# A fused attention and two-layer MoE kernel: the opening stage re-planned, with a shorter root for the norm

## The chip, the cores and the metric

The kernel runs on one core of a Trainium2 chip. The metric is device time in microseconds (us), the median of three runs. The profile is one further execution taken by the hardware profiler. The engines are PE (TensorE, the matmuls), DVE (VectorE), ACT (ScalarE), POOL (GpSimd) and SP (SyncE, which here issues the DMA transfers).

## The reference

Three layers follow each other. Linear attention over 4 batches, 8 heads, 576 positions and head size 64, with a norm over each head; then an expansion from 512 to 2048 features and back with an ELU between (`w_in`, `w_out`); then four experts of 1024 features weighted by probabilities (`w1`, `w2`).

```
kv  = einsum('bhsd,bhse->bhde', k, v)
out = einsum('bhsd,bhde->bhse', q, kv)
x   = out / sqrt(mean(out * out, axis=-1) + 1e-6) * g_norm     # per head
h   = x @ w_in;  g = where(h > 0, h, exp(min(h, 0)) - 1);  y = g @ w_out
out = sum_e p[:, e] * (max(y @ w1[e], 0) @ w2[e])               # p: probabilities over their sum
```

`w_in` and `w_out` arrive as 64-bit floats; the kernel converts them on the chip.

## The kernel before, in words

The 2304 tokens are 18 tiles of 128 rows, and six blocks (0 to 5) of three tiles. Large products are taken in three matmuls (high part by high, high by low, low by high) of float32r tiles, so every operand has to be split: ACT casts the high part (`nc.scalar.copy` in `split`), POOL subtracts it to get the low part.

For each block the opening stage does, in this order: `emit_o` (q times the kv of its batch, three PSUM banks, PE), `emit_square` (ACT), `emit_sum` and `emit_norm` (DVE: sum over a head, then the reciprocal root by a starting value in integer arithmetic and three Newton steps), `emit_scale` (DVE), `emit_xT` (PE transposes), `emit_x` (ACT writes the high part of the transposed block, DVE the low part). Then come `product1` (PE, one chunk of 128 features of `w_in`, 12 matmuls into bank a or b in turn), `begin_elu` (ACT), `end_elu` (DVE, which reads the bank of `product1` for the last time), `split_h` (ACT cast, POOL subtraction), and `half` (PE, 12 matmuls with `w_out` for two of the four output columns), whose banks `half_acc` copies out on ACT. Only chunks 0 and 1 of `w_in` and `w_out` are used in this stage. `emit_kv` accumulates k^T v of a tile (PE) and `emit_kvd` copies a batch's result out (ACT); `emit_o` of tiles 9 to 11 needs that of batch 2.

The conversion of a 64-bit chunk, `plan_float32`, has five pieces with places of their own: `begin_float32` (DVE, two instructions on the raw chunk, L151 and L154), `hold_exponent` (ACT, two), `add_low` (DVE, L168), `end_float32` (DVE, L176 and L179) and the split (ACT and POOL). Raw chunks lie in two buffers.

What sets the order: every piece is put into a list with a number (`at_place`), block j from 20 j on; the list is sorted and written out, and the instructions of PE, DVE, ACT and POOL are then tied to that order by dependencies that wait for nothing. Each of the four engines runs its instructions in that order. The order of SP's transfers is chosen by the scheduler. `busy(n)` gives PE n matmuls whose result nobody reads. After the opening stage come the other chunks of the expansion, with an order chosen by the scheduler, and then the experts.

Of the kernel before, what the change touches and what calls it, by code (L numbers as in the profile page):

```python
# [8 lines left out]
F32 = mybir.dt.float32  # L9
F32R = mybir.dt.float32r  # L10
AF = mybir.ActivationFunctionType
ALU = mybir.AluOpType
U32 = mybir.dt.uint32
# [11 lines left out]

@with_exitstack  # L30
def attention_moe_kernel(
# [14 lines left out]
    nc = tc.nc  # L46
    P = 128
    NT, DM = out.shape
    D, = g_norm.shape
    H = DM // D  # L50
# [12 lines left out]
    TT = T // P  # L63
# [26 lines left out]
    cv_p = layer1.enter_context(tc.tile_pool(name="cv", bufs=2, side="right"))  # L90
# [13 lines left out]
    g_sb = const.tile([P, 1], F32, name="g_sb")  # L104
    g8 = const.tile([P, 1], F32, name="g8")
# [40 lines left out]
    def begin_float32(r):  # L146
        r = r.rearrange("p (f t) -> p f t", t=2)
        w_low, w_high = r[:, :, 0], r[:, :, 1]
        m = cv_p.tile([P, 512], U32, tag="m", name="m")
        x = cv_p.tile([P, 512], U32, tag="x", name="x", bufs=1)  # L150
        nc.vector.tensor_scalar(  # L151
            out=x, in0=w_high, scalar1=20, scalar2=0x7FF, op0=ALU.logical_shift_right, op1=ALU.bitwise_and
        )
        nc.vector.tensor_scalar(  # L154
            out=m, in0=w_high, scalar1=0xFFFFF, scalar2=0x100000, op0=ALU.bitwise_and, op1=ALU.bitwise_or
        )
        return w_low, w_high, m, x
# [130 lines left out]
    at_p = at.enter_context(tc.tile_pool(name="at", bufs=2))  # L288
# [5 lines left out]
    for b in range(NKVD):  # L294
        t = at_p.tile([P, NHP, P], F32, tag=f"kvd{b}", name="kvd", bufs=1)
# [29 lines left out]
    ps_o, sums, xs = {}, {}, {}  # L325
# [24 lines left out]
    def emit_norm(j):  # L350


        s = sums[j]
        y, t = (at_p.tile([P, TT, H], F32, tag=n, name=n, bufs=1) for n in ("y", "t"))
        ts, tt, stt = nc.vector.tensor_scalar, nc.vector.tensor_tensor, nc.vector.scalar_tensor_tensor
        nc.vector.tensor_scalar_add(s, s, D * 1e-6)
        ts(out=y.bitcast(U32), in0=s.bitcast(U32), scalar1=-0.5, scalar2=float(0x5F3759DF), op0=ALU.mult, op1=ALU.add)
        for n in range(3):
            stt(out=t, in0=s, scalar=-0.5, in1=y, op0=ALU.mult, op1=ALU.mult)
            tt(out=t, in0=t, in1=y, op=ALU.mult)  # L360
            stt(out=s if n == 2 else y, in0=t, scalar=1.5, in1=y, op0=ALU.add, op1=ALU.mult)

    def emit_scale(t):

# [211 lines left out]
    def load_g():  # L576
        for o in (0, D):
            nc.sync.dma_start(out=g_sb[o:o + D], in_=g_norm.rearrange("(d o) -> d o", o=1))
        nc.gpsimd.tensor_scalar_mul(g8, g_sb, float(D)**0.5)

    def loads(text):
        for n in text.split():
# [10 lines left out]
    def at_place(place, op, *args):  # L593
        plan.append((place, len(plan), op, args))
# [3 lines left out]
    def plan_float32(ab, c, begins, holds, adds, ends, splits):  # L598
        def begin():
            load_w(0, ab, c)  # L600
            parts_of[ab, c] = begin_float32(raws[0, ab, c])

        def end():
            parts_of[ab, c] = end_float32(parts_of[ab, c])

        at_place(begins, begin)
        at_place(holds, lambda: hold_exponent(parts_of[ab, c]))
        at_place(adds, lambda: add_low(parts_of[ab, c]))
        at_place(ends, end)
        at_place(splits, lambda: split_w(0, ab, c, parts_of.pop((ab, c))))  # L610
# [22 lines left out]
    plan_norm(range(TT), [(-20, -19, -18, -10, -9.8, -7), (-19.5, -18.5, -17.5, -9.6, -8.8, -6),  # L633
                          (-19.2, -18.2, -17.2, -9.2, -7.8, -5)], ("abd", "fgh"))
    at_place(-16, emit_norm, 0)
    for place, op, n in ((-15, emit_kv, 5), (-14, emit_kv, 6), (-13, busy, 4), (-7.5, emit_kv, 7), (-7.4, emit_kv, 8)):
        at_place(place, op, n)
    at_place(-4.5, emit_kvd, 1)
    plan_float32(0, 1, -17.8, -17.1, -9, -4, -3.9)
# [3 lines left out]
    for j in range(NB):  # L643
        z = 20 * j
        if j + 1 < NB:
            plan_norm(range(TT * (j + 1), TT * (j + 2)), [
                (z, z + 1, z + 1.6, z + 6.5, z + 11.1, z + 11.4),
                (z + .9, z + 1.9, z + 2.5, z + 7.2, z + 11.6, z + 12.0),
                (z + 1.8, z + 2.8, z + 3.4, z + 7.9, z + 12.1, z + 12.6),
            ], ("dgh", "dgh"))  # L650
            at_place(z + 4.1, emit_norm, j + 1)
        first, second = ((2.7, 4.9, 8.4), (6.9, 8.3, 10.5)) if j else ((-.1, .3, 1.5), (6.9, 7.2, 8.2))
        for c, (mm, begins, ends) in enumerate((first, second)):
            at_place(z + mm, product1, j, c)
            at_place(z + begins, begin_elu, j, c)
            at_place(z + ends, end_elu, j, c)
            at_place(z + ends + (2 if j + c == 0 else 0), split_h, j, c)
        for t in more_kv.get(j, ()):
            at_place(z + 9, emit_kv, *t)
        if j in (1, 2):  # L660
            at_place(z + 9.3, emit_kvd, j + 1)
        if j:
            at_place(z + (4.8 if j > 1 else 12.6), half, j - 1, (0, 1))
            at_place(z + (6.5 if j > 1 else 12.65), half_acc, j - 1, (0, 1))
            at_place(z + 13.1, half, j - 1, (2, 3))
            at_place(z + 14.5, half_acc, j - 1, (2, 3))
        if j == NB - 2:
            at_place(z + 14, end_attention)
    plan_float32(1, 0, .1, 3, 12.7, 12.8, 12.9)
    plan_float32(1, 1, 28.9, 29, 29.1, 30.6, 30.61)  # L670
    plan_float32(0, 2, 48.9, 49, 49.1, 54, 54.1)
    plan_float32(0, 3, 68.9, 69, 69.1, 74, 74.1)
    plan_float32(1, 2, 100, 100.1, 100.2, 103, 103.1)
    plan_float32(1, 3, 108.9, 109, 109.1, 114, 114.1)
    z = 20 * NB
    at_place(z, half, NB - 1, (0, 1))
    at_place(z + 1, half_acc, NB - 1, (0, 1))
# [31 lines left out]
    for g, cs in list(enumerate(first_groups))[1:]:  # L709
        begins = 2 * len(steps)  # L710
# [17 lines left out]
    for h in range(2 * (len(steps) + LAG)):  # L728
        s, second = divmod(h, 2)
# [99 lines left out]
```

## Time and the profile before

| | |
|---|---|
| median of 3 runs | 1237.86 us (1237.55 to 1238.34) |
| the profiled execution, its own time | 1235.05 us |
| its span, first to last instruction | 1233.3 us |
| PE busy | 1207.3 us, 98% of the span |
| DVE, ACT, POOL busy | 51%, 36%, 28% |

The page of the profile gives busy time by engine and by groups of instructions; the trace behind it can be asked for waits, for stretches and for single instructions. Busy PE time counts matmuls at either of the two clock levels, so the granted clock is to be read beside it: 1.00 is 2.4 GHz and 0.50 is 1.2 GHz.

### The profile page before, as it was taken

Reading aid. Unit: us, or ns where it says so; the run is one execution under the profiler, and the core shown is the slowest. Engines: PE = TensorE matmul, PEld = TensorE weight load, DVE = VectorE, ACT = ScalarE, POOL = GpSimd, SP = SyncE. Lnnn points to the kernel's source line nnn. Section 1 sums busy time; section 2 is a strip of 40 time slices with the busy share of each in tenths; the row PEclk is TensorE's granted clock in tenths of the full one; section 3 lists DMA queues with packets and bytes.
Section 4 is the critical chain, followed back from the end, with each engine's and each line's share of the span. In section 5 each row is a group of like instructions: output and inputs, shape, how many; then the busy total and the mean of one; then the engine's idle time right before and its main releaser. Section 6 shows DMA issues by size and latency. Waiting matters only on the chain.

```text
span 1233.3 us, 16894 instructions
## 1 busy us (share of the span) xinstructions
PE 1207.3 (98%) x6656; PEld 1123.2 (91%) x6656; DVE 628.7 (51%) x1089; ACT 444.4 (36%) x858; POOL 339.9 (28%) x296
## 2 busy tenths in 40 slices
PE   8798999999999999999999999999999999999998
PEld 7698999999999999999999999999999999999997
DVE  5766897565222524855445445445444444444443
ACT  3566766544344443342122123123123123222110
POOL 1212444344233644343023023023023022121000
PEclk9799999999999999999999999999999999999999
DMA  9511323110000311542451451451551551550562
GB/s 333 206 44 52 89 84 103 52 52 18 1 10 12 137 66 45 230 155 57 179 192 47 178 203 37 185 205 35 188 205 35 188 200 34 193 197 18 205 231 77
DMA packets 43887, 147.14 MB, mean 119 GB/s; under 512 B 7072, under 2 KB 7072, under 8 KB 43808
## 3 DMA queue, kind: packets, MB, share of 16 engines
q1 hardware_dynamic: 43808, 146.07, 33.7%
q8 instruction: 52, 0.85, 0.3%
q14 instruction: 27, 0.22, 0.1%
HBM read 124.82 MB, written 21.23 MB: 118 GB/s over the span
## 4 chain that ended last, share of the span: by engine, by line
PE 84%; DVE 8%; DMA 3%; ACT 2%; issue 2%; POOL 1%; SPq 0%; DVEq 0%; ACTq 0%; POOLq 0%
PE ps_y L546 11%; PE ps_y L545 11%; PE ps_y L547 11%; PE ps_h L413 4%; PE ps_h L412 4%; PE ps_h L414 4%; PE ps_y L452 4%; PE ps_y L451 4%; PE ps_y L450 4%; PE ps_a L492 3%; PE ps_c L493 3%; PE ps_a L494 3%; PE ps_c L494 3%; PE ps_a L493 3%; PE ps_c L492 3%; PE ps_b L493 3%
## 5 line engine op out<-in xcount | busy, mean ns | idle before, releaser
L546 PE MATMUL ps_y<-w,h 128*128 128x512 f32 x576 | 226.2, 393 | 0.0
L545 PE MATMUL ps_y<-w,h 128*128 128x512 f32 x576 | 223.9, 391 | 0.4 <-DVE acc L558 0.4
L547 PE MATMUL ps_y<-w,h 128*128 128x512 f32 x576 | 220.2, 391 | 0.0
L531 DVE SCALAR_TENSOR_TENSOR h<-c,h 128x384 fp32r<-128x384 f32 x144 | 97.9, 680 | 135.7 <-ACT h L530 135.7
L519 POOL TENSOR_TENSOR c<-u,p 128x384 f32<-128x384 f32 x48 | 48.7, 1014 | 423.2 <-DVE h L531 423.2
L184 POOL TENSOR_TENSOR h<-e,h 128x384 fp32r<-128x384 f32 x96 | 101.1, 1055 | 200.2 <-ACT h L183 173.6
L530 ACT ACTIVATE h<-c 128x384 fp32r<-128x384 f32 x144 | 75.6, 525 | 202.2 <-POOL c L519 76.7
L412 PE MATMUL ps_h<-x,w 128*128 128x384 f32 x384 | 130.0, 339 | 3.8 <-DVE e L426 3.1
L413 PE MATMUL ps_h<-x,w 128*128 128x384 f32 x384 | 128.6, 335 | 0.9 <-DVE x L388 0.9
L452 PE MATMUL ps_y<-h,w 128*128 128x384 f32 x384 | 129.1, 337 | 0.3 <-POOL w L184 0.3
L451 PE MATMUL ps_y<-h,w 128*128 128x384 f32 x384 | 129.0, 336 | 0.0
L450 PE MATMUL ps_y<-h,w 128*128 128x384 f32 x384 | 123.3, 338 | 5.3 <-ACT w L183 4.3
L414 PE MATMUL ps_h<-x,w 128*128 128x384 f32 x384 | 128.4, 334 | 0.0
L547 PEld LDWEIGHTS ps_y<-w,h 128*128 128x128 f32 x576 | 108.1, 188 | 21.7
L545 PEld LDWEIGHTS ps_y<-w,h 128*128 128x128 f32 x576 | 108.0, 188 | 19.5 <-DVE acc L558 0.8
L546 PEld LDWEIGHTS ps_y<-w,h 128*128 128x128 f32 x576 | 108.0, 188 | 19.5
L558 DVE SCALAR_TENSOR_TENSOR acc<-ps_y,p_sb,acc 128x512 f32<-128x512 f32 x126 | 87.6, 746 | 65.2 <-PE ps_y L547 64.9
L426 DVE SCALAR_TENSOR_TENSOR e<-e,ps_h 128x384 f32<-128x384 f32 x96 | 52.5, 548 | 115.1 <-ACT e L422 112.7
L421 ACT ACTIVATE e<-ps_h 128x384 f32<-128x384 f32 x96 | 46.8, 487 | 93.0 <-PE ps_h L414 89.1
L412 PEld LDWEIGHTS ps_h<-x,w 128*128 128x128 f32 x384 | 72.1, 188 | 6.9 <-DVE e L426 5.9
L508 ACT COPY p<-ps_c 128x384 f32<-128x384 f32 x48 | 23.1, 481 | 153.2 <-PE ps_c L494 153.2
L450 PEld LDWEIGHTS ps_y<-h,w 128*128 128x128 f32 x384 | 72.2, 189 | 6.3 <-ACT w L183 4.6
(103 smaller groups left out, 2375.7 us busy)
## 6 DMA issues: line engine op xcount, KB each, us to landing
f<-kept SPq DMA_DIRECT2D x98, 768.0 KB, 7.6
raw<-in_moe_w_dram SPq DMA_DIRECT2D x64, 256.0 KB, 2.7
kept<-f SPq DMA_DIRECT2D x21, 768.0 KB, 3.8
raw<-in_moe_w_in_dram SPq DMA_DIRECT2D x16, 512.0 KB, 3.7
raw<-in_moe_w_out_dram SPq DMA_DIRECT2D x16, 512.0 KB, 3.6
qkv<-in_k_dram SPq DMA_DIRECT2D x18, 256.0 KB, 5.7
qkv<-in_v_dram SPq DMA_DIRECT2D x18, 256.0 KB, 5.8
qkv<-in_q_dram SPq DMA_DIRECT2D x18, 256.0 KB, 5.8
```

The lines of the kernel that those rows point to most:

```text
L184: eng.tensor_tensor(out=lo, in0=src, in1=hi.bitcast(F32), op=ALU.subtract)
L412: nc.tensor.matmul(ps, ah, bh, start=(kk == 0), stop=False)
L413: nc.tensor.matmul(ps, ah, bl, start=False, stop=False)
L414: nc.tensor.matmul(ps, al, bh, start=False, stop=(kk == KD - 1))
L450: nc.tensor.matmul(ps, bh[:, cols], hi, start=first, stop=False)
L451: nc.tensor.matmul(ps, bh[:, cols], lo, start=False, stop=False)
L452: nc.tensor.matmul(ps, bl[:, cols], hi, start=False, stop=last)
L493: nc.tensor.matmul(ps, wh, xl, start=False, stop=False, skip_group_check=True)
L531: nc.vector.scalar_tensor_tensor(out=lo, in0=ps, scalar=0.0, in1=hi.bitcast(F32), op0=ALU.max, op1=ALU.subtract,)
L545: nc.tensor.matmul(ps, hi[:, cols], bh, start=first, stop=False)
L546: nc.tensor.matmul(ps, hi[:, cols], bl, start=False, stop=False)
L547: nc.tensor.matmul(ps, lo[:, cols], bh, start=False, stop=last)
```

## The change

The root takes two Newton steps in place of three (another starting value, constants that make up for it, a factor in `g8`), and its two scratch tiles become slices of the tile of squares. The scratch tile `x` of the conversion has two buffers in place of one. The rest is places: two more idle-time `busy` calls are set in block 0 (9, and 6 in place of 4); in blocks 0 and 1 `emit_kv` comes ahead of the transposes; the transposes (`emit_xT`) and `emit_x` come about two places earlier; `split_h` has a place of its own, behind `emit_x`; the second `end_elu` of a block comes behind `emit_x`; in block 0 the first one does too. Both early chunks of `w_out` are converted in block 0; before, the second one was converted in block 1.

```
-        x = cv_p.tile([P, 512], U32, tag="x", name="x", bufs=1)
+        x = cv_p.tile([P, 512], U32, tag="x", name="x")
...
-        y, t = (at_p.tile([P, TT, H], F32, tag=n, name=n, bufs=1) for n in ("y", "t"))
+        y, t = (xs[TT * j + TT - 1][:, n:n + TT, :H] for n in (0, TT))
...
-        ts(out=y.bitcast(U32), in0=s.bitcast(U32), scalar1=-0.5, scalar2=float(0x5F3759DF), op0=ALU.mult, op1=ALU.add)
-        for n in range(3):
-            stt(out=t, in0=s, scalar=-0.5, in1=y, op0=ALU.mult, op1=ALU.mult)
+        ts(out=y.bitcast(U32), in0=s.bitcast(U32), scalar1=-0.5, scalar2=float(0x5F1FFFF9), op0=ALU.mult, op1=ALU.add)
+        for scale, add, into in ((-1.0, ROOT_ADD, y), (-0.5 * ROOT_MUL**2, 1.5, s)):
+            stt(out=t, in0=s, scalar=scale, in1=y, op0=ALU.mult, op1=ALU.mult)
             tt(out=t, in0=t, in1=y, op=ALU.mult)
-            stt(out=s if n == 2 else y, in0=t, scalar=1.5, in1=y, op0=ALU.add, op1=ALU.mult)
+            stt(out=into, in0=t, scalar=add, in1=y, op0=ALU.add, op1=ALU.mult)
...
-    for place, op, n in ((-15, emit_kv, 5), (-14, emit_kv, 6), (-13, busy, 4), (-7.5, emit_kv, 7), (-7.4, emit_kv, 8)):
+    for place, op, n in ((-15.5, busy, 9), (-15, emit_kv, 5), (-14, emit_kv, 6), (-13, busy, 6),
+                         (-7.5, emit_kv, 7), (-7.4, emit_kv, 8)):
...
-                (z, z + 1, z + 1.6, z + 6.5, z + 11.1, z + 11.4),
-                (z + .9, z + 1.9, z + 2.5, z + 7.2, z + 11.6, z + 12.0),
-                (z + 1.8, z + 2.8, z + 3.4, z + 7.9, z + 12.1, z + 12.6),
+                (z, z + 1, z + 1.6, z + 6.5, z + 9.0, z + 10.4),
+                (z + .9, z + 1.9, z + 2.5, z + 7.2, z + 9.2, z + 10.8),
+                (z + 1.8, z + 2.8, z + 3.4, z + 7.9, z + 9.4, z + 11.2),
...
-        first, second = ((2.7, 4.9, 8.4), (6.9, 8.3, 10.5)) if j else ((-.1, .3, 1.5), (6.9, 7.2, 8.2))
+            (2.7, 4.9, 8.4, 11.4) if j else (-.1, 3.5, 11.6, 11.6), (6.9, 10 if j else 8.3, 11.5, 11.7)
...
-            at_place(z + ends + (2 if j + c == 0 else 0), split_h, j, c)
+            at_place(z + splits, split_h, j, c)
         for t in more_kv.get(j, ()):
-            at_place(z + 9, emit_kv, *t)
+            at_place(z + (9.8 if j > 1 else 8.95), emit_kv, *t)
         if j in (1, 2):
-            at_place(z + 9.3, emit_kvd, j + 1)
+            at_place(z + 12, emit_kvd, j + 1)
         if j:
-            at_place(z + (4.8 if j > 1 else 12.6), half, j - 1, (0, 1))
-            at_place(z + (6.5 if j > 1 else 12.65), half_acc, j - 1, (0, 1))
+            at_place(z + (4.8 if j > 1 else 8.9), half, j - 1, (0, 1))
+            at_place(z + (6.5 if j > 1 else 10.3), half_acc, j - 1, (0, 1))
...
-    plan_float32(1, 0, .1, 3, 12.7, 12.8, 12.9)
-    plan_float32(1, 1, 28.9, 29, 29.1, 30.6, 30.61)
-    plan_float32(0, 2, 48.9, 49, 49.1, 54, 54.1)
-    plan_float32(0, 3, 68.9, 69, 69.1, 74, 74.1)
+    plan_float32(1, 0, .1, 4.6, .2, 11.45, 11.5)
+    plan_float32(1, 1, .3, 4.7, 11.46, 11.47, 11.8)
+    plan_float32(0, 2, 48.9, 51.6, 49, 53.9, 54)
+    plan_float32(0, 3, 68.9, 71.6, 69, 73.9, 74)
     plan_float32(1, 2, 100, 100.1, 100.2, 103, 103.1)
-    plan_float32(1, 3, 108.9, 109, 109.1, 114, 114.1)
+    plan_float32(1, 3, 108.9, 109, 109.1, 114, 114.6)
```

Three places of the order carry the argument. The first is DVE between block 0's low parts and block 1's sums. Before (`raw_130` is chunk 1 of `w_in`, `raw_258` chunk 0 of `w_out`, `sq_400` block 1's first tile of squares, `e_388` the ELU of block 0's first chunk):

```order
L176 SCALAR_TENSOR_TENSOR x_265<-raw_130,x_265 128x512
L179 SCALAR_TENSOR_TENSOR m_264<-m_264,x_265 128x512
L151 TENSOR_SCALAR x_385<-raw_258 128x512
L154 TENSOR_SCALAR m_384<-raw_258 128x512
L426 SCALAR_TENSOR_TENSOR e_388<-e_388,ps_h_355 128x384
L348 TENSOR_REDUCE ss_403<-sq_400 128x8
```

In the change, where all lines are three or four further down (`raw_380` is chunk 1 of `w_out`, `sq_409` block 1's first tile of squares):

```order
L179 SCALAR_TENSOR_TENSOR x_265<-raw_130,x_265 128x512
L182 SCALAR_TENSOR_TENSOR m_264<-m_264,x_265 128x512
L154 TENSOR_SCALAR x_392<-raw_258 128x512
L157 TENSOR_SCALAR m_391<-raw_258 128x512
L171 SCALAR_TENSOR_TENSOR m_391<-raw_258,m_391 128x512
L154 TENSOR_SCALAR x_397<-raw_380 128x512
L157 TENSOR_SCALAR m_396<-raw_380 128x512
L351 TENSOR_REDUCE ss_411<-sq_409 128x8
```

The first two instructions on chunk 1 of `w_out` now stand ahead of block 1's sums, and the first ELU's end is gone from here. The order of SP's transfers up to this chunk is the same in both kernels; it is its 45th.

The second place is DVE behind block 1's scaling. Before (`ps_xT_506` is the last transposed tile of block 1, `e_449` the second ELU of block 0, `sq_529` block 2's first tile of squares):

```order
L366 TENSOR_TENSOR sq_413<-ps_o_405,ss_403 128x512
L426 SCALAR_TENSOR_TENSOR e_449<-e_449,ps_h_435 128x384
...
L388 SCALAR_TENSOR_TENSOR x_496<-ps_xT_506,g8_93,x_496 128x4x128
L168 SCALAR_TENSOR_TENSOR m_384<-raw_258,m_384 128x512
L176 SCALAR_TENSOR_TENSOR x_385<-raw_258,x_385 128x512
L179 SCALAR_TENSOR_TENSOR m_384<-m_384,x_385 128x512
L348 TENSOR_REDUCE ss_531<-sq_529 128x8
```

In the change (`ps_xT_493` is that last tile, `e_424` and `e_455` are the first and the second ELU of block 0):

```order
L392 SCALAR_TENSOR_TENSOR x_507<-ps_xT_493,g8_93,x_507 128x4x128
L179 SCALAR_TENSOR_TENSOR x_392<-raw_258,x_392 128x512
L182 SCALAR_TENSOR_TENSOR m_391<-m_391,x_392 128x512
L171 SCALAR_TENSOR_TENSOR m_396<-raw_380,m_396 128x512
L179 SCALAR_TENSOR_TENSOR x_397<-raw_380,x_397 128x512
L182 SCALAR_TENSOR_TENSOR m_396<-m_396,x_397 128x512
L430 SCALAR_TENSOR_TENSOR e_455<-e_455,ps_h_440 128x384
L430 SCALAR_TENSOR_TENSOR e_424<-e_424,ps_h_362 128x384
L351 TENSOR_REDUCE ss_545<-sq_543 128x8
```

Both ends of block 0's ELUs now stand behind five conversion instructions; the bank that `e_424` reads is the one that block 1's first `product1` writes next.

The third place is ACT around block 4's high parts (the x written from ps_xT). Before:

```order
L421 ACTIVATE e<-ps_h 128x384
L422 ACTIVATE e<-e 128x384
L183 CAST h<-e 128x384
L162 ACTIVATE x<-x,ebias 128x512
L163 ACTIVATE x<-x,ebias 128x512
L183 CAST h<-e 128x384
L387 ACTIVATE x<-ps_xT,g_93 128x4x128 x3
```

In the change:

```order
L425 ACTIVATE e<-ps_h 128x384
L426 ACTIVATE e<-e 128x384
L391 ACTIVATE x<-ps_xT,g_93 128x4x128 x3
L186 CAST h<-e 128x384
L165 ACTIVATE x<-x,ebias 128x512
L166 ACTIVATE x<-x,ebias 128x512
L186 CAST h<-e 128x384
```

The two casts of h, the second of which needs the end of an ELU on DVE, and the two conversion instructions have moved from ahead of the high parts to behind them.

## Rows read from the trace of the kernel before

**Rows 1.** Busy time by engine in three stretches; then granted clock, DMA.

```profile
36.00:64.00 28.00, 20.71 (x128) 18.74 (x129) 19.77 (x39) 13.39 (x25) 5.54 (x5) 0.76 0.44 155
64.00:112.00 48.00, 44.37 (x356) 41.60 (x355) 34.45 (x80) 30.39 (x59) 8.60 (x8) 1.00 0.13 39
112.00:300.00 188.00, 185.59 (x1058) 182.89 (x1058) 133.27 (x227) 112.92 (x217) 81.86 (x70) 1.00 0.23 71
```

**Rows 2.** PE's waits between 36 and 64 us: in total, times, longest.

```profile
PE ps_y L450 <- ACT w L183: 4.3, 1, 4.3
```

**Rows 3.** PE's waits between 64 and 112 us.

```profile
PE ps_o L334 <- DVE x L388: 2.3, 1, 2.3
PE ps_h L413 <- DVE x L388: 0.5, 1, 0.5
PE ps_h L412 <- ACT x L387: 0.4, 1, 0.4
```

**Rows 4.** Busy time in two stretches of 2 us; third from the end the clock.

```profile
38.00:40.00 2.00, 1.41 (x8) 0.83 (x7) 0.84 (x2) 1.13 (x3) 0.54 (x1) 0.66 1.03 377
44.00:46.00 2.00, 2.00 (x13) 2.00 (x13) 0.82 (x2) 1.62 (x4) 1.27 (x1) 0.64 0.45 131
```

**Rows 5.** SP's queue: start, duration, transfer.

```profile
32.05 0.33 SPq L137 DMA_DIRECT2D raw<-in_moe_w_out_dram  x1
```

**Rows 6.** DMA issues between 32.0 and 32.5 us: size, us to landing.

```profile
raw<-in_moe_w_out_dram SPq DMA_DIRECT2D x1, 512.0 KB, 5.9
```

**Rows 7.** DVE in order of time: start, us, line, operation, count, idle before.

```profile
28.41 0.42 DVE L154 TENSOR_SCALAR m<-raw 128x512 uint32<-128x512 uint32 x1
...
40.00 2.07 DVE L388 SCALAR_TENSOR_TENSOR x<-ps_xT,g,x 128x512 fp32r<-128x512 f32 x3 [1.17 <-ACT x L387]
...
42.59 0.68 DVE L176 SCALAR_TENSOR_TENSOR x<-raw,x 128x512 uint32<-128x512 uint32 x1
...
51.59 0.54 DVE L426 SCALAR_TENSOR_TENSOR e<-e,ps_h 128x384 f32<-128x384 f32 x1
...
52.84 1.47 DVE L168 SCALAR_TENSOR_TENSOR m<-raw,m 128x512 f32<-128x512 uint32 x1
...
83.30 1.87 DVE L348 TENSOR_REDUCE ss<-sq 128x8 f32<-128x512 f32 x3 [1.95 <-ACT sq L341]
85.20 0.18 DVE L356 TENSOR_SCALAR ss<-ss 128x24 f32<-128x24 f32 x1
...
87.66 1.89 DVE L366 TENSOR_TENSOR sq<-ps_o,ss 128x512 f32<-128x512 f32 x3
```

**Rows 8.** PE in order of time.

```profile
37.24 2.17 PE L377 MATMUL ps_xT<-ident,sq 128*128 128x128 f32 x12 [1.62 <-DVE sq L366]
40.81 5.14 PE L334 MATMUL ps_o<-kvd,qkv 128*128 128x128 f32 x24 [1.40 <-DVE x L388]
45.71 0.42 PE L412 MATMUL ps_h<-x,w 128*128 128x384 f32 x1
...
50.05 1.30 PE L315 MATMUL ps_kv<-qkv 128*64 128x64 f32 x32
...
64.03 2.84 PE L334 MATMUL ps_o<-kvd,qkv 128*128 128x128 f32 x24
...
75.67 1.53 PE L377 MATMUL ps_xT<-ident,sq 128*128 128x128 f32 x12
...
88.40 1.85 PE L377 MATMUL ps_xT<-ident,sq 128*128 128x128 f32 x12
```

**Rows 9.** ACT in order of time.

```profile
53.97 0.73 ACT L322 COPY kvd<-ps_kv 64x256 f32<-64x256 f32 x2
...
92.69 0.51 ACT L183 CAST h<-e 128x384 fp32r<-128x384 f32 x1 [0.76 <-DVE e L426]
93.10 1.84 ACT L387 ACTIVATE x<-ps_xT,g 128x512 fp32r<-128x512 f32 x3
```

**Rows 10.** POOL in order of time.

```profile
52.76 1.01 POOL L184 TENSOR_TENSOR h<-e,h 128x384 fp32r<-128x384 f32 x1 [6.77 <-ACT h L183]
```

More of the change, by code (lines that the diff above doesn't have):

```diff
@@ L14 @@
 AX = mybir.AxisListType
+ROOT_MUL, ROOT_ADD = 0.703952253, 2.38924456
 @with_exitstack
@@ L578, in load_g @@
             nc.sync.dma_start(out=g_sb[o:o + D], in_=g_norm.rearrange("(d o) -> d o", o=1))
-        nc.gpsimd.tensor_scalar_mul(g8, g_sb, float(D)**0.5)
+        nc.gpsimd.tensor_scalar_mul(g8, g_sb, float(D)**0.5 * ROOT_MUL * (1 + 3.26e-7))
     def loads(text):
@@ L646, in attention_moe_kernel @@
             plan_norm(range(TT * (j + 1), TT * (j + 2)), [
-                (z, z + 1, z + 1.6, z + 6.5, z + 11.1, z + 11.4),
-                (z + .9, z + 1.9, z + 2.5, z + 7.2, z + 11.6, z + 12.0),
-                (z + 1.8, z + 2.8, z + 3.4, z + 7.9, z + 12.1, z + 12.6),
+                (z, z + 1, z + 1.6, z + 6.5, z + 9.0, z + 10.4),
+                (z + .9, z + 1.9, z + 2.5, z + 7.2, z + 9.2, z + 10.8),
+                (z + 1.8, z + 2.8, z + 3.4, z + 7.9, z + 9.4, z + 11.2),
             ], ("dgh", "dgh"))
             at_place(z + 4.1, emit_norm, j + 1)
-        first, second = ((2.7, 4.9, 8.4), (6.9, 8.3, 10.5)) if j else ((-.1, .3, 1.5), (6.9, 7.2, 8.2))
-        for c, (mm, begins, ends) in enumerate((first, second)):
+        for c, (mm, begins, ends, splits) in enumerate((
+            (2.7, 4.9, 8.4, 11.4) if j else (-.1, 3.5, 11.6, 11.6), (6.9, 10 if j else 8.3, 11.5, 11.7)
+        )):
             at_place(z + mm, product1, j, c)
```

## The prediction

> **What bounds the kernel now.** I read the stretches first. PE is busy in almost all of the span, and behind 112 us it stands for 2.4 us of 188 [rows 1]; so the change can only win what PE loses ahead of that, and lose by making PE stand. From 36 to 64 us PE is busy for 20.7 of 28 us, and its mean clock is 0.76: (1 - 0.76) / 0.5 x 28 = 13.4 us lie at the lower level, where each matmul takes twice as long. From 64 to 112 us the clock is 1.00 and PE stands for 3.6 us. Then I read what PE waits for: up to 64 us for the cast of `w_out` chunk 1 (4.3 us, its conversion ends too late, [rows 2]) and for the scaled tile of block 1 (1.62, [rows 8]); from 64 to 112 us chiefly for the parts of x: 2.3, 0.5 and 0.4 [rows 3]. Last I followed the chain of single instructions on DVE, ACT and PE through blocks 0 to 5; the steps below come from there.
>
> **Block 1: the wait that the change makes.** It lets DVE begin `w_out` chunk 1 ahead of block 1's sums. That chunk's transfer is issued at 32.05 and lands 5.9 us later, at 38.0 [rows 5, 6]. Its place on SP is the same in the change, and the DMA engines are still full at 38 to 40 us (share 1.03, [rows 4]), so I take 38.0 again. DVE is past chunk 0's first pair at 28.8 [rows 7]; with the new `add_low` (0.7) it stands from about 30 to 38. Behind the waiting instruction are block 1's sums, root and scaling, and for these PE waits. What block 0 gains or loses ahead of that (three root instructions less, 11 more `busy` matmuls) is swallowed: whichever way, DVE is at the transfer in time.
>
> The Trainium skill ("TensorE: Matmul & The Clock Gate", engine queue depths) says that Vector and Scalar queues are strictly first in, first out and only TensorE pulls weight loads ahead. By that nothing passes the waiting instruction, which speaks against the change; the sum as worked out here is the same, and without the rule it would be that of the hidden transfer below. No row here shows an overtaking on DVE.
>
> From 38.0, with durations from [rows 7] unless said:
> - the pair on chunk 1, 2 x 0.42: 38.8; three sums, 1.9: 40.7
> - the root: 11 instructions take 87.66 - 85.20 = 2.46, so 8 take 1.8: 42.5. The strided slices cost nothing, as the low part, which is written in pieces of 128, costs 0.69 a tile, like the plain 128x512 (0.68). Were each to cost double, it would be 1.8 more
> - the first scaled tile, 0.6, and 0.1 to PE: 43.2. PE has then stood since 35.6 (before, until 37.24, [rows 8]), and the clock has fallen: after that shorter stand it fell at 38.6 (a mean of 0.66 from 38 to 40) and came back at 45.4 (0.64 from 44 to 46) [rows 4]
> - transposes at the low clock: 24 records of `emit_o` took 5.14 there [rows 8], so 12 take 2.6: 45.8
> - last high part 0.6 [rows 9], low part 0.7, handing over 0.3: 47.4
> - conversions in between: five instructions of about 0.7, and 0.6 because one falls beside POOL's split of chunk 0 (beside POOL such an instruction took 1.47, [rows 7, 10]): 51.5
> - two ends of ELUs, 0.5 each: 52.5
>
> Only now is bank a free for block 1's `product1`. PE has done `emit_o` (24 records at 5.14 / 24 = 0.21 while the clock is low, at 2.84 / 24 = 0.12 behind, [rows 8]) by about 49.5, and stands once more, for about 3 us. Before, that product began at 45.71 [rows 8]. So here the change is 6.8 us late.
>
> It then gets most of this back, since the 4.3 us wait and the low stretch around it are gone. Two products last 50.05 - 45.71 = 4.3 [rows 8], so half of one pair is 2.1. From 52.5: two products 56.8, `half` 58.9, k^T v 1.2 (1.30 with its tail): 60.1, where block 2's transposes begin. Chunk 1 of `w_out` is split by 56.6 (its cast is behind two of h, and POOL needs about 1.0 for each piece, [rows 10]), in time. Behind the transposes stands a new wait: `emit_o` of tiles 9 to 11 needs batch 2's copy, which now lies on ACT behind three high parts and both casts of h, the second of which needs an ELU's end behind the low parts. That is 0.8 to the first high part (a third of 1.53 for the tile, [rows 8], and handing over), 1.8 for three, 0.8 for the last low part, 0.5 for the ELU, 0.5 for the cast, 0.7 for the copy [rows 7, 9]: 5.2, against 3.6 of PE work. So `emit_o` starts at 65.3 with a full clock, against 64.03 [rows 8]: **+1.3**.
>
> The clock: before, it stayed up over a stand of 2.3 us [rows 1, 3] and fell over the 4.3 [rows 1, 2]. A stand of 3 us, short after a low stretch, lies between; I take it as falling, being third in a row of gaps. The low stretches before lasted 6.7 us (two in 13.4); of the one after the stand about half falls on work, 3.2 us, which costs half of that: **+1.6**. Bounds: 0 (no fall) and 3.4 (all 6.8 on work). So `emit_o` of block 3 starts at 66.9, 2.9 late.
>
> **Blocks 3 to 5: the waits that the change takes away.** Before, ACT ran block 4's high parts at 93.10, behind a cast that had waited for an ELU [rows 9], while their transposes had been there since 88.4 to 90.3 [rows 8]. The change puts high and low parts directly behind the transposes, with 2.1 us of `half` between them and their user, and k^T v as well behind the transposes of block 3. High parts and low parts are done 3.4 us after the transposes begin (0.8 + 1.8 + 0.8); transposes and `half` take 1.5 + 2.1 = 3.6. So the waits of [rows 3] go, and with them the 3.6 us in which PE stood [rows 1]. A stop also costs the overlap of matmuls (24 start 4.34 / 24 = 0.18 apart, while the one after a stop lasts 0.42, [rows 8]): 0.2 for each of some four stops, 0.7. The transposes of blocks 4 and 5 were drawn out by waits within them, 1.85 against 1.53 [rows 8]: 2 x 0.32 = 0.6. Together **-5.0** (bounds: -2.5 if the waits are only halved, and -5.0, for no more can go). The shorter root is worth nothing here: PE's other work covers it, as the scaled tile is ready about 1 us ahead of the transposes. Were that cover gone it would be 0.65 a block.
>
> **Behind 112 us.** The scheduler's order changes in many places. PE stands there for 2.4 us while DVE is busy for 133 of 188 [rows 1], and a second `x` buffer lets DVE's conversions overlap: bounds -2.4 and, with DVE worse placed, the same standing half as long again, +1.2; I take **-0.6**, nearer to nothing since DVE's work stays the same.
>
> **Sum.** 1.3 + 1.6 - 5.0 - 0.6 = -2.7. Of the profiled execution's 1235.05 us (span 1233.3 and 1.75 around it) that leaves 1232.35; it ran 2.8 below the median, which goes to 1237.86 - 2.7 = **1235.2**.
>
> **The rivals.**
> - *No second fall of the clock.* The stand before block 1's products is met at full clock: 1.6 less, 1233.6. For it: 2.3 us did not make it fall. Against: the stand is longer. 0.15.
> - *The transfer is hidden.* If chunk 1 lands by 31, block 1's scaled tile is there at 37.2 as before [rows 8] and not at 43.2, 6.0 earlier: 1229.2. Against it stands the landing at 38.0 on full DMA engines. 0.05.
> - *The clock stays low through blocks 1 and 2* (the other side). The stands before the transposes, before the products and before block 3's `emit_o` follow each other; if the clock does not return between them, work of 11 us runs at half speed. Each us of it beyond my 3.2 costs what it would have taken: up to 8 more, 1243; from 5.1 more on the kernel is slower than before by over 0.2%. For it: 13.4 us at the low level before, with fewer stands. Against: full PE work brought the clock back at 45.4. 0.15. The Trainium skill (the same page, on oscillation of the clock in real kernels) says that gaps let the array fall back to half rate and that each burst then starts cold. By that this rival gains weight; the trace agrees in its two low stretches [rows 1, 4].
> - *The waits of blocks 3 to 5 only move.* The ELU's first end and `begin_float32` still stand ahead of the low parts on DVE; if high and low parts come 1 us later than reckoned, half of the 5.0 stays: 1237.7. 0.20.
>
> **How the numbers follow.** Forecast 0.45, with its own range 1233.6 to 1236.8. A measurement of this kernel tells about 0.2%, 2.5 us, from no change: faster is below 1235.4, slower above 1240.3. Of the forecast 0.27 lies below 1235.4 and 0.18 above. Faster: 0.27 + 0.15 + 0.05 = 0.47; the same: 0.18 + 0.20 = 0.38; slower 0.15. The range takes in the first rival, the fourth and the near part of the third: 1231.6 to 1240.0, leaving out the hidden transfer and most of the third.
>
> **What would show it.** Right: DVE standing until about 38 on an instruction that reads raw, PE standing 7 us ahead of block 1's transposes and 3 us ahead of its products, a wait for the kvd copy ahead of tile 9, none for the cast of `w_out`, block 3's `emit_o` starting at 65 to 67, no wait for x from there to 112. Wrong: a landing far from 38.0 (each us moves the sum by a us), or waits for x in blocks 3 to 5 as long as before.

## The result, and the profile after

The changed kernel takes 1251.73 us (median of 4 runs, 1251.02 to 1252.9) against 1238.01 for the kernel before beside it: a ratio of 1.0112, 95% interval 1.0094 to 1.0130. The profiled execution took 1251.88 us, its span is 1250.1. It is slower by 1.1%, where 1235.2 had been forecast.

Three stretches of the changed kernel, with the columns of [rows 1] (PE, PEld, DVE, ACT, POOL busy, clock, DMA):

```profile
36.00:64.00 28.00, 18.32 (x127) 17.51 (x128) 20.57 (x44) 13.11 (x24) 4.92 (x5) 0.82 0.38 136
64.00:112.00 48.00, 45.58 (x368) 43.89 (x368) 35.80 (x74) 31.50 (x63) 10.74 (x10) 1.00 0.14 39
112.00:300.00 188.00, 173.95 (x952) 166.44 (x951) 137.60 (x213) 105.46 (x203) 81.25 (x65) 0.98 0.23 71
```

The opening came out much as forecast in its sum; the loss lies in the last row. Behind 112 us PE is busy for 173.95 us of 188 instead of 185.59, and DVE is busy for longer than before (137.6 against 133.3) with fewer instructions (213 against 227). What PE waits for there (total, times, longest; `acc` is the running sum of the second product, which DVE adds to). The kernel before waited in this stretch 1.2 us in 3 waits for an ELU's end and 1.0 in 2 for `acc`:

```profile
PE ps_h L416 <- DVE e L430: 9.8, 13, 1.3
PE ps_y L454 <- DVE acc L448: 3.4, 5, 1.8
PE ps_y L455 <- POOL h L187: 0.8, 1, 0.8
```

Two marks locate the loss. The first matmul of block 4's first `half` (columns 0 and 1, behind block 5's first product) starts at 109.81 against 111.65: up to there the change has won 1.84 us. The first matmul of the experts starts at 492.0 against 475.4. So the rest of the expansion takes 382.2 us instead of 363.8, **18.4 more**, and the experts take what they took (1250.1 - 492.0 = 758.1 us to the end of the span, against 1233.3 - 475.4 = 757.9). The stretch between the two marks, before and in the change (columns as above):

```profile
111.65:475.45 363.80, 359.43 (x2058) 356.09 (x2058) 187.81 (x317) 186.65 (x361) 153.50 (x131) 1.00 0.18 58
109.81:492.00 382.19, 366.19 (x2058) 358.04 (x2057) 200.72 (x319) 186.70 (x363) 158.39 (x131) 0.99 0.17 55
```

For the same matmuls PE stands for 16.0 us instead of 4.4, and DVE is busy for 12.9 us longer.

The opening. DVE in order of time (start, us, line, operation, count, idle before and its releaser), to set beside the steps of the prediction:

```profile
28.45 0.69 DVE L171 SCALAR_TENSOR_TENSOR m<-raw,m 128x512 f32<-128x512 uint32 x1
36.94 0.43 DVE L154 TENSOR_SCALAR x<-raw 128x512 uint32<-128x512 uint32 x1 [7.80 <-DMA raw<-in_moe_w_out_dram]
...
37.62 1.86 DVE L351 TENSOR_REDUCE ss<-sq 128x8 f32<-128x512 f32 x3
39.52 0.18 DVE L360 TENSOR_SCALAR ss<-ss 128x24 f32<-128x24 f32 x1
...
41.31 1.89 DVE L370 TENSOR_TENSOR sq<-ps_o,ss 128x512 f32<-128x512 f32 x3
...
48.96 1.63 DVE L182 SCALAR_TENSOR_TENSOR m<-m,x 128x512 f32<-128x512 f32 x1
50.52 1.00 DVE L430 SCALAR_TENSOR_TENSOR e<-e,ps_h 128x384 f32<-128x384 f32 x2
```

PE in order of time (transposes of block 1, `emit_o` of block 2, first product of block 1, k^T v, `emit_o` of block 3, which answers to 64.03 in [rows 8]):

```profile
42.06 2.82 PE L381 MATMUL ps_xT<-ident,sq 128*128 128x128 f32 x12 [6.76 <-DVE sq L370]
44.74 3.30 PE L337 MATMUL ps_o<-kvd,qkv 128*128 128x128 f32 x24
51.67 0.41 PE L416 MATMUL ps_h<-x,w 128*128 128x384 f32 x1 [3.62 <-DVE e L430]
...
59.65 1.30 PE L318 MATMUL ps_kv<-qkv 128*64 128x64 f32 x32
...
66.06 2.94 PE L337 MATMUL ps_o<-kvd,qkv 128*128 128x128 f32 x24 [1.56 <-ACT kvd L325]
```

Windows of 2 us; the clock is third from the end. It falls while PE stands for DVE, comes back on the work behind, and falls a second time after the stand of 3.6 us:

```profile
38.00:40.00 2.00, 0.00 (x0) 0.00 (x0) 1.90 (x6) 1.75 (x4) 0.00 (x0) 0.67 1.06 382
44.00:46.00 2.00, 2.00 (x13) 1.74 (x12) 1.79 (x3) 1.38 (x2) 0.00 (x0) 0.62 0.00 0
52.00:54.00 2.00, 2.00 (x9) 2.00 (x8) 0.47 (x1) 2.00 (x6) 1.86 (x2) 0.59 0.62 251
54.00:56.00 2.00, 2.00 (x8) 2.00 (x8) 1.90 (x6) 1.07 (x3) 1.36 (x2) 0.56 0.00 0
56.00:58.00 2.00, 2.00 (x14) 2.00 (x13) 1.72 (x8) 0.69 (x2) 0.00 (x0) 1.00 0.00 0
```

Behind 112 us, DVE's groups from 112 to 240 us (operation, shapes, count, busy us, mean ns, idle before):

```profile
L179 DVE SCALAR_TENSOR_TENSOR x<-raw,x 128x512 uint32<-128x512 uint32 x22 | 21.7, 988 | 3.1 <-ACT x L166 3.1
L171 DVE SCALAR_TENSOR_TENSOR m<-raw,m 128x512 f32<-128x512 uint32 x20 | 18.5, 929 | 0.2
L182 DVE SCALAR_TENSOR_TENSOR m<-m,x 128x512 f32<-128x512 f32 x21 | 17.4, 835 | 0.0
...
L154 DVE TENSOR_SCALAR x<-raw 128x512 uint32<-128x512 uint32 x22 | 15.8, 720 | 5.8 <-DMA raw<-in_moe_w_out_dram 4.0 <-DMA raw<-in_moe_w_in_dram 1.6
...
L430 DVE SCALAR_TENSOR_TENSOR e<-e,ps_h 128x384 f32<-128x384 f32 x26 | 14.1, 544 | 9.3 <-ACT e L426 9.3
```

The same groups of the kernel before have means of 760, 789, 716, 641 and 545 ns. The instructions of a conversion have become longer, the end of an ELU has not: (988 - 760) x 22 + (929 - 789) x 20 + (835 - 716) x 21 + (720 - 641) x 22 = 12 us more of DVE in 128 us. Counted in the timelines of DVE and POOL over the same stretch, 30 of 62 conversion instructions with two inputs (L171, L179, L182) overlap a subtraction of POOL in the change, and 12 of 62 before. Those that overlap none take 0.67 to 0.69 us in both kernels; those that do take up to 1.78 and 1.51. One place, DVE from 163 to 171 us:

```profile
163.57 0.53 DVE L430 SCALAR_TENSOR_TENSOR e<-e,ps_h 128x384 f32<-128x384 f32 x1
164.04 1.70 DVE L179 SCALAR_TENSOR_TENSOR x<-raw,x 128x512 uint32<-128x512 uint32 x1
165.65 1.49 DVE L171 SCALAR_TENSOR_TENSOR m<-raw,m 128x512 f32<-128x512 uint32 x1
...
167.87 0.68 DVE L182 SCALAR_TENSOR_TENSOR m<-m,x 128x512 f32<-128x512 f32 x1
```

and POOL there:

```profile
163.91 1.28 POOL L187 TENSOR_TENSOR w<-m,w 128x512 fp32r<-128x512 f32 x1 [4.54 <-ACT w L186]
165.14 1.46 POOL L187 TENSOR_TENSOR h<-e,h 128x384 fp32r<-128x384 f32 x1
```

The two DVE instructions that lie beside POOL's subtractions take 1.70 and 1.49 us; the next one shown with two inputs of this size, with POOL idle, takes 0.68. PE's own record of the place: it had waited 1.78 us for `acc` up to 161.37, its clock had fallen (mean 0.91 from 160 to 200 us), and it stood 0.65 more for the ELU's end at 163.57.

### The profile page after: what moved, and what is told of

Its sections match the earlier page's. It is cut to its first block, busy times and chain, and to the rows that moved or that the text cites. A ratio compares the mean times of both kernels' runs of the same rounds, so it can differ in the third digit from the quotient of the medians.

```text
span 1250.1 us, 16912 instructions
## 1 busy us (share of the span) xinstructions
PE 1212.9 (97%) x6678; PEld 1126.8 (90%) x6678; DVE 639.1 (51%) x1071; ACT 443.1 (35%) x858; POOL 346.6 (28%) x296
## 4 chain that ended last, share of the span: by engine, by line
PE 82%; DVE 10%; DMA 4%; ACT 2%; issue 1%; SPq 0%; POOL 0%; DVEq 0%; ACTq 0%
PE ps_y L550 11%; PE ps_y L549 11%; PE ps_y L551 11%; PE ps_h L416 4%; PE ps_h L417 3%; PE ps_h L418 3%; PE ps_y L455 3%; PE ps_y L456 3%; PE ps_y L454 3%; PE ps_a L496 3%; PE ps_a L498 3%; PE ps_a L497 3%; PE ps_c L497 3%; PE ps_c L498 3%; PE ps_c L496 3%; PE ps_b L497 3%
## 5 line engine op out<-in xcount | busy, mean ns | idle before, releaser
L187 POOL TENSOR_TENSOR h<-e,h 128x384 fp32r<-128x384 f32 x96 | 105.1, 1096 | 216.0 <-ACT h L186 185.2
L416 PE MATMUL ps_h<-x,w 128*128 128x384 f32 x384 | 132.1, 344 | 15.4 <-DVE e L430 15.4
L417 PE MATMUL ps_h<-x,w 128*128 128x384 f32 x384 | 130.0, 339 | 0.5 <-DVE x L392 0.5
L418 PE MATMUL ps_h<-x,w 128*128 128x384 f32 x384 | 129.8, 338 | 0.0
L430 DVE SCALAR_TENSOR_TENSOR e<-e,ps_h 128x384 f32<-128x384 f32 x96 | 52.5, 548 | 130.0 <-ACT e L426 126.0
```

Of the source, the lines that this page charges most:

```text
L187: eng.tensor_tensor(out=lo, in0=src, in1=hi.bitcast(F32), op=ALU.subtract)
L416: nc.tensor.matmul(ps, ah, bh, start=(kk == 0), stop=False)
L417: nc.tensor.matmul(ps, ah, bl, start=False, stop=False)
L418: nc.tensor.matmul(ps, al, bh, start=False, stop=(kk == KD - 1))
```

## The experiments

Two theories were set against each other first. A: the second buffer of `x` makes the loss; the scheduler may begin a conversion while the last is open, so DVE's queue and its work beside POOL get worse for the ends of ELUs, for which PE waits. The rival: the buffer is innocent, and the scheduler draws another order because the opening hands over at another moment. The kernel before ran beside each group of runs (medians 1235.8, 1235.9 and 1236.5), and ratios are to it.

**One buffer behind the opening.** The changed kernel, with the second buffer for chunk 1 of `w_out` alone, so that the opening stays as it is:

```diff
-    def begin_float32(r):
+    def begin_float32(r, tag="x"):
-        x = cv_p.tile([P, 512], U32, tag="x", name="x")
+        x = cv_p.tile([P, 512], U32, tag=tag, name="x", bufs=1)
-            parts_of[ab, c] = begin_float32(raws[0, ab, c])
+            parts_of[ab, c] = begin_float32(raws[0, ab, c], "x2" if (ab, c) == (1, 1) else "x")
```

> The change, but the second x buffer belongs to chunk 1 of w_out alone; every conversion behind the opening stage has one x buffer again, as before the change. If the second buffer causes the 18 us lost behind 112 us (it lets the scheduler begin a conversion while the last one is still open, and the ends of ELUs queue on DVE behind both), the time is 1235 to 1238, and PE's waits for the ends of ELUs behind 112 us fall from 9.8 to about 1 us. If the loss comes from the scheduler having drawn another order because the opening stage hands over at another moment, it is 1248 to 1253.

Measured: 1235.09 us, ratio 0.9993 (0.9984 to 1.0003). Block 3's `emit_o` starts at 66.15 (66.06 in the changed kernel), the `half` at 109.91, the experts at 475.2: the opening is that of the change, the loss behind it is gone. PE's waits from 112 to 300 us:

```profile
PE ps_y L454 <- DVE acc L448: 2.1, 4, 1.0
PE ps_h L416 <- DVE e L430: 0.6, 2, 0.4
```

So 1.2% of the time, 15 us, hangs on this one buffer. The rival falls: the opening hands over at the same moment as in the changed kernel.

**The short root alone, and with the second buffer.** In the change the short root, with its scratch slices, comes together with the second buffer. So the kernel before was run with the root's part of the change alone, and with the root and the buffer. No places are changed in either. The second is the first with:

```diff
-        x = cv_p.tile([P, 512], U32, tag="x", name="x", bufs=1)
+        x = cv_p.tile([P, 512], U32, tag="x", name="x")
```

> The kernel before with the two-step root alone, as a control for the kernel with two x buffers. Both theories: 1236 to 1238.5, since three instructions less shorten the chain of blocks 0 to 2 by 0.65 us each where PE waits for the scaled tile, and PE's work hides them behind.

> The kernel before with the short root and its slices (which make room for it), and two x buffers; no place is changed. Second buffer: 1250 to 1256, with waits for the ends of ELUs between 112 and 300 us as in the change. Order drawn anew by the opening: 1236 to 1239, like the kernel with the short root alone.

Measured: 1232.51 us, ratio 0.9968 (0.9959 to 0.9977), for the root alone, and 1245.71 us, ratio 1.0080 (1.0065 to 1.0095), with the buffer: 13.2 us for the buffer, in a kernel with the old opening. (Both lie below the expected times; the gap between them is what tells the theories apart.) The experts begin at 473.0 and 486.3. With the buffer PE waits, from 112 to 300 us:

```profile
PE ps_h L415 <- DVE e L429: 6.2, 9, 1.5
PE ps_y L453 <- DVE acc L447: 4.0, 7, 0.9
```

That settles theory A from the other side. The root alone was a surprise: I had put it at nothing. Its stretch from 36 to 64 us:

```profile
36.00:64.00 28.00, 19.77 (x135) 17.46 (x132) 18.96 (x35) 13.20 (x26) 5.57 (x5) 0.88 0.42 146
```

The clock is 0.88 there, against 0.76 in [rows 1]: the low level lasts (1 - 0.88) / 0.5 x 28 = 6.7 us instead of 13.4. The first of the two low stretches is missing, and block 2's `emit_o`, 5.14 us in [rows 8], takes 2.94. In these traces the gain does not come from there, though. `emit_o` of blocks 3 and 5:

```profile
63.75 2.84 PE L337 MATMUL ps_o<-kvd,qkv 128*128 128x128 f32 x24
...
93.05 2.95 PE L337 MATMUL ps_o<-kvd,qkv 128*128 128x128 f32 x24 [1.36 <-DVE x L391]
```

Block 3's starts only 0.3 us ahead of the 64.03 of [rows 8]: in between PE stands longer for the cast of `w_out` chunk 1 (4.7 us against 4.3), and from the end of that stand to this `emit_o`, mostly at the low level, it takes 7.2 us against 6.4. From there to block 4's first `half`, at 109.39, PE takes 45.6 us instead of 47.6 (45.6 in two_x_before too): the wait ahead of block 5's `emit_o` falls from 2.3 to 1.4 us, and the one for block 5's scaled tile (0.4) is gone. By that mark 2.3 of the 2.4 us are won by which the experts begin earlier. One execution of each does not show that the root keeps the clock up, either: the mean clock of whole executions lay between 0.993 and 0.997 in the 21 executions of the kernel before beside this run, and between 0.993 and 0.997 in the ten of the short root. Yet each of the 21 took longer (1233.80 us or more) than any of the ten (1233.26 or less).

So in these traces the root alone gains no less up to that mark than the whole change (2.3 us against 1.84), and the kernel with it alone (1232.51 us) is 2.6 us faster than the one that has the changed places as well and one buffer behind the opening (one_x_late, 1235.09).

**The opening without the stand, first try.** one_x_late, with chunk 1 of `w_out` begun behind block 1's scaling instead of ahead of its sums:

```diff
-    plan_float32(1, 1, .3, 4.7, 11.46, 11.47, 11.8)
+    plan_float32(1, 1, 8, 8.1, 11.46, 11.47, 11.8)
```

> The kernel with one late x buffer, and DVE begins chunk 1 of w_out behind block 1's scaling in place of ahead of its sums. The stand of DVE for that transfer (7.8 us in the change) should go, and with it PE's 6.8 us ahead of block 1's transposes: block 3's emit_o starts 5 to 7 us earlier than the 66.1 of the change. Second buffer: 1229 to 1232. Order drawn anew: 1242 to 1247. If the stand was not on the path, no difference to the kernel with one late x buffer.

Measured: 1231.07 us, ratio 0.9965 (0.9953 to 0.9978), block 3's `emit_o` at 62.55. Less than hoped, because the stand has only moved. Transposes and `emit_o` of block 2 on PE:

```profile
35.07 1.85 PE L381 MATMUL ps_xT<-ident,sq 128*128 128x128 f32 x12 [0.28 <-DVE sq L370]
43.15 5.49 PE L337 MATMUL ps_o<-kvd,qkv 128*128 128x128 f32 x24 [6.23 <-DVE x L392]
```

and ACT between them:

```profile
39.33 0.72 ACT L165 ACTIVATE x<-x,ebias 128x512 uint32<-128x512 uint32 x1 [5.25 <-DVE x L154]
...
41.64 1.83 ACT L391 ACTIVATE x<-ps_xT,g 128x512 fp32r<-128x512 f32 x3
```

ACT's part of the conversion (place 8.1) stands ahead of block 1's high parts (L391) and waits for the same transfer; the high parts, ready since the transposes at 35 to 37, wait behind it.

**The opening without the stand, second try.** one_x_late, with that chunk begun behind block 1's low parts, ACT's part too, and block 0's ends of ELUs right behind the low parts:

```diff
-            (2.7, 4.9, 8.4, 11.4) if j else (-.1, 3.5, 11.6, 11.6), (6.9, 10 if j else 8.3, 11.5, 11.7)
+            (2.7, 4.9, 8.4, 11.4) if j else (-.1, 3.5, 11.25, 11.6), (6.9, 10 if j else 8.3, 11.5 if j else 11.26, 11.7)
-    plan_float32(1, 1, .3, 4.7, 11.46, 11.47, 11.8)
+    plan_float32(1, 1, 11.3, 11.32, 11.46, 11.47, 11.8)
```

> The kernel one_x_late, with two edits in block 0: w_out chunk 1 is begun behind block 1's low parts instead of ahead of its sums, and block 0's two ends of ELUs go on DVE right behind those low parts, ahead of all conversions. If the opening is bound by what DVE and ACT have queued behind the transfer, nothing of block 1's norm stands behind it any more: scaled tile for block 1's transposes at about 35, no wait of 6 to 8 us between 30 and 50, block 2's emit_o starting at about 39 to 40 at the full clock, block 3's at 55 to 59 (62.55 in one_x_no_stand), and a ratio of 0.991 to 0.995 to before. Rival, the transfers bound the opening: q, k and v land no earlier, the stand only moves to the next product or k^T v, block 3's emit_o stays at 61 to 63 and the ratio at 0.996 to 0.998.

Measured: 1224.03 us, ratio 0.9901 (0.9884 to 0.9919), a version that beats both kernels. PE from the transposes of block 1 on:

```profile
35.32 1.85 PE L381 MATMUL ps_xT<-ident,sq 128*128 128x128 f32 x12 [0.27 <-DVE sq L370]
37.54 2.94 PE L337 MATMUL ps_o<-kvd,qkv 128*128 128x128 f32 x24 [0.37 <-DVE x L392]
40.24 0.42 PE L416 MATMUL ps_h<-x,w 128*128 128x384 f32 x1
...
57.06 2.94 PE L337 MATMUL ps_o<-kvd,qkv 128*128 128x128 f32 x24 [1.57 <-ACT kvd L325]
```

The stands of 6.8 and 3.6 us are gone, and block 3's `emit_o` comes 9.1 us earlier than in one_x_late (66.15). The experts begin at 465.65, 9.6 us earlier, so nothing of it is given back. The rival of this run, that the transfers bind the opening, falls. The low clock is nearly gone too: over the whole execution the mean clock is 0.998 to 1.0 in the four executions, against 0.992 to 0.997 in the kernel before.

**The copy of kvd earlier.** late_chunk1 with one place changed:

```diff
-            at_place(z + 12, emit_kvd, j + 1)
+            at_place(z + 11.3, emit_kvd, j + 1)
```

> late_chunk1 with the copy of kvd for batches 2 and 3 ahead of the casts of h on ACT (place 11.3 instead of 12). The wait for that copy ahead of block 3's emit_o was 1.6 in the changed kernel and in one_x_late: if it is still there in late_chunk1, it goes here, and the time is 1 to 2 us less than late_chunk1's; if PE's other work covers it by then, no difference (within 0.5 us).

Measured: 1224.30 us, ratio 0.9911 (0.9895 to 0.9926), the same as late_chunk1 within the intervals. The wait is gone as expected, `emit_o` comes 1.4 us earlier and takes a little less:

```profile
55.62 2.84 PE L337 MATMUL ps_o<-kvd,qkv 128*128 128x128 f32 x24
```

but the experts begin only 0.6 us earlier (465.01). The expected 1 to 2 us did not come. By block 5's transposes 0.9 us of the 1.4 is left (94.04 against 94.98); why it shrinks was not followed.

**What in the second buffer costs.** Two mechanisms remained within theory A. Queue: an ELU's end stands behind instructions of two open conversions. Contention: the conversions now lie beside POOL's splits and take longer. POOL's subtraction for the first layer's weights from chunk 2 on was replaced by zeros, which POOL only writes (these low parts are left out of the result), in all four kernels, with one buffer and with two:

```diff
-        split(w[:, 0, :], w[:, 1, :], r, nc.gpsimd)
+        if layer == 0 and n > 1:
+            nc.scalar.copy(w[:, 0, :], r)
+            nc.gpsimd.memset(w[:, 1, :].bitcast(F32), 0.0)
+        else:
+            split(w[:, 0, :], w[:, 1, :], r, nc.gpsimd)
```

> short_root_before (one x buffer) with the same low parts written as zeros by POOL and left out of the result: the base for two_x_memset. Both theories expect 1225 to 1233 here (the ratio to before 0.990 to 0.998): PE has few waits behind 112 us to lose. Theory contention expects two_x_memset within 4 us of it, theory queue 9 to 15 us above it.

> two_x_before (the kernel before with the short root and two x buffers), in which POOL writes zeros as the low parts of the first layer's weights from chunk 2 on, instead of subtracting (those low parts are left out of the result, so its output is off by them). POOL reads nothing for these pieces, so DVE's conversions no longer meet its splits. Theory contention (the second buffer costs 13 us since conversions stand in pairs beside POOL's splits and take up to 1.3 us each): DVE's mean of L176 and L179-like conversions from 112 us falls to about 0.70, and the gap to short_root_memset is under 4 us. Theory queue (it costs since ends of ELUs stand behind two open conversions, whatever these take): the gap stays 9 to 15 us, with waits for ps_h on DVE's ends of ELUs of 5 to 10 us again from 112 us on.

> one_x_late with the same low parts written as zeros and left out of the result: the one-buffer base for after_memset. PE's order is nearly that of one_x_late, so both theories expect 1231 to 1237 (ratio to before 0.996 to 1.001).

> The changed kernel, in which POOL writes zeros as the low parts of the first layer's weights from chunk 2 on instead of subtracting (those low parts are left out of the result). The same edit moved the one-buffer kernel of the pair before by +0.5% through a redrawn order, so that pair alone doesn't settle the share. Contention (DVE's conversions beside POOL's splits): 1234 to 1241 here, the gap to one_x_late_memset under 5 us, the conversions' means from 112 to 240 us back to 0.70 to 0.80. Queue (ends of ELUs stand behind two open conversions, whatever these take): 1244 to 1251, gap 10 to 17 us.

| | one buffer | two buffers | the buffer's cost |
|---|---|---|---|
| old places | 0.9968 | 1.0080 | 1.12% |
| old places, zeros written | 1.0021 (1.0011 to 1.0030) | 1.0015 (1.0006 to 1.0025) | -0.06% |
| new places | 0.9993 | 1.0112 | 1.19% |
| new places, zeros written | 1.0024 (1.0013 to 1.0035) | 1.0034 (1.0024 to 1.0044) | 0.10% |

Medians: 1238.44 and 1237.74 us, 1239.31 and 1240.62 us. In both pairs the buffer's cost vanishes with POOL's subtractions, as contention expected. Queue's gaps of 9 to 17 us did not come, nor did its long waits: from 112 to 300 us PE waits for ELU ends for 1.6 us in two_x_memset and 3.3 in after_memset, against 6.2 and 9.8 with the subtractions. The five DVE instructions of a conversion (L154, L157, L171, L179 and L182 in the change) take together, from 112 to 240 us (count times mean), 73, 72 and 75 us in the kernels with one buffer (before, short_root_before, one_x_late), 85 and 86 with two (two_x_before, after), and 73 to 74 in all four with zeros. So the lengthening comes with the second buffer and goes with the subtractions. Not every group falls to the 0.70 us that contention expected: L179 takes 797 ns in two_x_memset and 875 in after_memset. From 112 to 300 us, the changed kernel with zeros:

```profile
112.00:300.00 188.00, 181.42 (x1022) 176.28 (x1021) 127.34 (x221) 112.45 (x213) 61.21 (x68) 1.00 0.24 71
```

and one_x_late with zeros:

```profile
112.00:300.00 188.00, 183.09 (x1030) 178.96 (x1029) 133.56 (x225) 111.50 (x214) 58.67 (x68) 0.99 0.23 70
```

PE wins back 7.5 us in the first against the changed kernel (173.95), DVE is busy for 10 us less with 8 instructions more. But the one-buffer kernels became slower with the zeros, by 0.5% and 0.3% (1238.44 and 1239.31 us, where 1225 to 1233 and 1231 to 1237 had been expected): the scheduler drew another order for them, in which PE waits more (5.6 us for `acc` and 1.2 for ELU ends in short_root_memset, against 1.1 and 0.9). So the gaps close from both sides: the two-buffer kernels become faster by 0.65% and 0.78%, the one-buffer kernels slower by 0.53% and 0.31%. A redrawn order seems to be worth 4 to 6 us by itself, though no run changes the order alone, and this test gives the direction and not the exact share. Queue isn't ruled out as a part: from 112 to 200 us an ELU's end started on DVE on average 1.8 us after ACT had it ready in the changed kernel, with zeros too (1.8), against 1.1 before and 1.3 in one_x_late. POOL's time also shrinks with the zeros (0.53 us a piece instead of 1.3 to 1.5), which these runs don't tell from the stretched DVE instructions.

## Why the prediction was wrong

By its own steps, in order.

- **The wait in block 1: right.** The transfer was issued 1.1 us earlier than taken (30.95 against 32.05), and landed 6.0 later; DVE stood until 36.94, not 38.0. From there each step took what was reckoned: eight root instructions 1.79 us (1.8; the strided slices cost nothing), transposes at the low clock 2.7 from start to start (2.6), ELU ends at 51.5 (52.5), block 1's product at 51.67 after a stand of 3.6 (3). The conversion beside POOL was lengthened by 0.95 (0.6 taken).
- **The second fall of the clock: right.** 0.59 and 0.56 in two windows of 2 us are (0.41 + 0.44) / 0.5 x 2 = 3.4 us at the low level, all on work, which cost 1.7 (1.6). It was a choice between two values all the same: in [rows 4, 8] the clock had fallen after a stand of 1.62 us, and over 2.3 us it had stayed up [rows 1, 3], so the length of the stand alone did not tell.
- **The new wait for kvd, and block 3's `emit_o`: right.** 1.56 us of waiting, where the sum gave 5.2 - 3.6 = 1.6 (its terms add up to 5.1), and 66.06 against 66.9, earlier because the transfer landed earlier.
- **Blocks 3 to 5: right in kind, too large in size.** From block 3's `emit_o` to the mark at 109.81 PE takes 43.75 us instead of 47.62: 3.9 won and not 5.0. Behind 66 us 0.9 of the 3.6 is left, a wait for block 5's scaled tile. It was there before, as the fourth of PE's waits from 64 to 112 us, which [rows 3] does not show:

```profile
PE ps_xT L377 <- DVE sq L366: 0.4, 1, 0.4
```

At the mark the change stands at -1.84; the three terms had given 1.3 + 1.6 - 5.0 = -2.1. That these agree so well is in part luck: +2.0 instead of +2.9 ahead of block 3's `emit_o` and -3.9 instead of -5.0 behind it nearly cancel.
- **"The shorter root is worth nothing here": wrong.** The reason given was that the scaled tile is ready about 1 us ahead of the transposes; block 5's transposes wait for it. In the kernel before, the root alone gains 0.3%, 2.0 us of it in this stretch (45.6 instead of 47.6). How much of the 3.9 is the root's in the change, and how much the places', no run tells apart.
- **"Behind 112 us", -0.6 with bounds -2.4 and +1.2: the step that failed.** It measured +18.4. The words were that "a second `x` buffer lets DVE's conversions overlap" and that "DVE's work stays the same". What the runs showed in its place: this buffer by itself costs 13 to 15 us (one_x_late, two_x_before), and DVE's work does not stay the same: more of its conversions lie beside POOL's subtractions, a group's mean rises by up to 30% (988 against 760 ns), and DVE is busy for 200.7 us instead of 187.8 with 319 instructions instead of 317. The bound was taken from the time for which PE stood before, which says how much can be won and nothing about how much can be lost. And "DVE is busy for 133 of 188" was a mean over unequal parts: from 112 to 160 us it was 38.7 of 48 before, so a few us more filled it; in the changed kernel it is busy for 39.7 of 40 from 160 to 200 us. The 18.4 are 11.6 us more in which PE stands (16.0 against 4.4) and 6.8 more in which it is busy with the same matmuls (366.2 against 359.4). Of the 6.8 at most 3.6 is the clock of 0.91 from 160 to 200 us (0.09 x 40); the rest was not followed. It does not lie behind 300 us, where 1095 matmuls take 192.0 us in the change and 1000 took 175.45 before.

Of the rivals none came true. The one on the slower side put the loss on the clock in blocks 1 and 2; the place was wrong as well as the mechanism, and its 1243 us is still some 9 short of the measured time.

The Trainium skill ("SBUF — State Buffer", "Who interferes with whom") says that a DVE instruction with two SBUF inputs contends with a GpSimd instruction that reads SBUF, and not with one that only writes. The trace agrees: 1.70 and 1.49 us beside POOL's subtraction and 0.68 without, while the four such instructions that lie beside POOL's writing of zeros and beside no subtraction (two each in two_x_memset and after_memset, from 112 to 240 us) take 0.68 to 0.69. No step of the prediction priced it behind 112 us.

## What to carry to other kernels

A buffer that lifts a dependency is not free where the order is left to a scheduler: price it at the engine that it lets run ahead, by that engine's busy share in the fullest stretch, not over the whole, and bound the loss by the work that may be lengthened, not by the waits that are there now. Where a wait for a transfer stands in one in-order queue, look for the same transfer's user in the other queues: moving it on DVE alone only moved the stand to ACT. Once that chunk was behind everything that PE waits for, places and shorter root together were worth 1% (0.9901), of which the root alone gives 0.3% (0.9968); as they stood in the change, with one buffer behind the opening, the two gave nothing (0.9993). A part of a change that is put at nothing is worth a run by itself.

## What the runs showed of the hardware

DVE instructions with one SBUF input were lengthened too. DVE in the changed kernel:

```profile
124.91 1.12 DVE L154 TENSOR_SCALAR x<-raw 128x512 uint32<-128x512 uint32 x1 [1.63 <-DMA raw<-in_moe_w_out_dram]
125.96 1.23 DVE L157 TENSOR_SCALAR m<-raw 128x512 uint32<-128x512 uint32 x1
```

and POOL at that time:

```profile
123.20 2.55 POOL L187 TENSOR_TENSOR w<-m,w 128x512 fp32r<-128x512 f32 x2 [1.88 <-ACT w L186]
125.71 1.20 POOL L187 TENSOR_TENSOR h<-e,h 128x384 fp32r<-128x384 f32 x1
```

Alone, these two take 0.42 to 0.43 us (36.94 above). In the changed kernel the 24 instructions of this kind from 112 to 240 us that overlap no subtraction take 0.41 to 0.43 us, and the 18 that overlap one take 1.01 on average, up to 1.52. The time that PE's clock spends at its low level is not the same in each execution of one kernel: the mean clock of the kernel before, over whole executions, lay between 0.992 and 0.997.
